# Feed-forward weights in 256-KB pieces, column form for any group, and a new written-out order

## The chip, the core and the metric

The kernel runs on one core of one Trainium2 chip. The metric is the device time of one execution in microseconds. PE is TensorE (matrix products), ACT is ScalarE, DVE is VectorE, POOL is GpSimd, and SP is the queue from which the large loads and stores are issued. A matrix product is two instructions, a load of the stationary operand and the matmul.

## The reference

A transformer block with conditioning: six modulation vectors come from `c`, then attention with 32 query heads and one shared key and value head, then a gated feed-forward, each behind a layer norm. S = 2048 positions, D = 1024, F = 3584, heads of 32, in bf16.

```python
mod = (_silu(c) @ w_mod).reshape(c.shape[0], 6, 1, -1)     # sa, ca, ga, sb, cb, gb
h = _layernorm(x) * (1 + ca) + sa
q = (h @ wq) in 32 heads of 32;  k = h @ wk;  v = h @ wv   # one k and v for all heads
p = softmax(q k^T / sqrt(32));   x = x + ga * ((p v) @ wo)
h = _layernorm(x) * (1 + cb) + sb
x = x + gb * ((_silu(h @ w1) * (h @ w3)) @ w2)
```

## The kernel before

**Tiling.** The positions are cut into 8 blocks of 256 (`NB`), the heads into 8 groups of four. For each block and each group of heads 8 *score groups* (`s_exp`) are made: eight matmuls of 32 rows write a pair of key tiles for four heads into four PSUM banks, and ACT takes the exponential of each half (128x1024), from a ring of three pairs of banks into `U`. There are 512 score groups and 1,024 exponentials. `av` multiplies them by V (128x32 tiles, "A" form), DVE adds them up for the denominators (`pairs`, into `PS`), and `dens` and `attend` divide. When a block has all its heads, `wo` projects it and adds it to `X1`, a layer norm follows, and for blocks 2 to 6 a DMA transpose on SP turns the result around.

**Feed-forward.** `ffn1` runs over 14 slabs of 256 columns of w1 and w3. `slab_dma` loads both parts of a slab from SP into one of three slots (`W13SL`; two of them lie in `W13`, one in `HT`), `slab` multiplies them with the block's layer norm output; ACT takes a tanh, DVE forms the gated product into `HHT`. `ffn2` runs over four quarters of 256 output columns: `w2_dma` loads 28 x 128 rows of w2 into one of two slots (`W2S`; for the last block's third and fourth quarter into `QT` and `U`), `quarter` makes 56 products. All feed-forward weights are loaded again for each of the eight blocks. The feed-forward of one block lies between the score groups of the next; after the last score group only products of the last blocks are left.

**Forms of a product.** A 128x128 product can be issued whole ("F") or as four products of 32 columns at four column positions ("C", four times the instructions). A change between score form "S", narrow forms "A" and "C", and F costs PE some time; A and C go together. In the kernel before, products of `slab`, `q_proj` and `wo` may take form C: `mode_of` gives it when PE stands in A or C, at most `COLS` (12) products after the last A and while an estimated instruction load stays under `FULL`. All pairs of products that go to one group share one list `form`, so the first pair decides for the group. `quarter` has form F alone.

**Order.** `program` builds a graph of operations with their reads and writes. `Placer` puts them on engines; `ORDER` lists all operations by number, so each engine's instruction order is fixed in the text (a "b" marks the second of two possible engines), and each engine waits for semaphores where an operation depends on another engine. The times in `Placer` (`SWITCH`, `LAT` and others) then decide only which PSUM bank a group takes and whether filler matmuls are put into expected gaps of PE.

Of the kernel before, what the change touches and what calls it, by code (L numbers as in the profile page):

```python
# [8 lines left out]
P = 128  # L9
# [110 lines left out]
6 1 11 0 4 2 5 8 3 7 9 12 13 10 25 16-18 59 22 15 14 60 19 61 28 21 62 412 63 27 20 23 64 24 65 26 29 68 30 31 36 45  # L120
37 32 66 33 38 69 39 40 103 67 34 102 41 35 70 104 131 105 71 123 42 72 132 73 122 106 74 43 124 112 107 46 125 44
133 75 126 47 48 134 108 49 135 50 76 136 111 109 127 113 77 137 128b 114 110b 115 129 116 130 117b 78 118 79 80 119
99 172 81 82 171 97 55b 54 53 51 85 58 98b 57 52b 56 173 163 83 86b 174 162 175 138 84 164 182 87 176 139 88 165 89
143 90 166 91 92 142 167 93 94 168 95 183 140 96 144 460 152 145 141b 120 146 151 461 169 153 147 121 462 154 148b
463 155 170b 464 149 156 184 242 185 157b 150 186 177b 421 191 465 187 158 243 192 178 159 193 188b 466 194 179b 195
467 160 202 196 468 197b 469 180 161 470 203 198 181 471 204 472 199b 205 189 473 206 211 100 190b 207 474 475 101
208b 227 477 228 212 229 230 200 476 231 213 244 214 209 215 201b 245 478 246 210 216 232 233 247 234 235 217b 479
222 236 223 248 224 225 480 218 249 226 481 219 250 252 253 251 254 255 487 482 257-260 483 256 501 261 220 502 485
237 503 504 221 238 488 239 505 240 262 263 506 241 484 507 491-493 489 494 508 264 265 509 495 510 266 496 497 511
486 498 499 267 268 512 500 513 490 269 514 270 526 307 515 516 308 517 271 309 310 525 518 519 272 520 311 273 274  # L130
528 521 522 275 523 527 302 303 524 276 562 304 563 305 529-531 564 565 306 532 533 566 541 538 539 567 277 540 568
542 534 543 569 535-537 544 278 570 548 571 553 545 572 546 552 279 547 280 573 549 574 550 297 281 575 298 551 299
# [4 lines left out]
640 646-648 661 649 652 650 662 357 663 680 358 359 664 651 665 360 681 666 327 361 328 667 653 668 654 332 669 333  # L137
682 334 670 335 655 671 336 329 672 330 683 322 673 331 674 323 675 684 324 325 676 677 326 337 678 338 685 413 679
703 414 430 339 418 704 417 415 340 416 686 688 705 706 689 690 707 687 691-693 341 694 708 695 709 699 696 710 697
# [8 lines left out]
834 835 930 836 931 1313 840 1314 828 837 1315 457 411 838 1316 839 1317 458 841 1318 842 843 846-848 1319 459 1320  # L148
# [3 lines left out]
911-913 1369 1335 914 915 1370 916 1336 917 918 890 1383 919 972 891 892 1371 1372 893 920 894 895 1373 896 1340 897  # L152
921 951 922 1338 898 1375 1374 923 899 924-926 1341 1376 927 928 900 1342 973 901 1377 902 1378 1386 903 904 1379
905 906 929 907 1380 952 1406 908 1351 1408 1381 932-934 1407 935 936 1352 937 938 1387 939 1392 940 993 1354 1393
1384 1409 1394 1355 1410 1395 1396 941 1397 1398 1411 1399 1356 1412 1388 942 1413 943-945 1402 946 1414 947 1389
1415 948 1382 949 1416 953 1390 994 954-956 1417 950 1418 957 1385 958 1419 959 960 844 1432 963 1014 964 961 965
1421 1420 966 962 967 968 1433 969 1422 970 974 1391 1015 975 976 1423 971 1424 977 978 845 1425 979 1435 980 981
984 982 1035 985 1427 1426 1436 986 987 983 988 989 1428 990 991 995 992 1036 996 1429 997 1455 1400 1456 998 1401
999 1000 1430 1001 1457 1002 1016 1056 1017 1458 1437 1003 1018 1019 1459 1020-1022 1004 1023 1460 1461 1431 1077
1441 1442 1024 1403 1443 1434 1444 1462 1445 1025 1446-1448 1404 1463 1464 1438 1005 1006 1465 1007 1405 1008 1439  # L160
1009 1010 1466 1011 1451 1467 1440 1012 1468 1026 1481 1057 1027-1030 1469 1470 1013 1031 1032 1471 1482 1033 1037
1078 1038 1034 1039 1472 1040 1473 1041 1474 1042 1484 1043 1044 1047 1045 1098 1048 1476 1475 1485 1049-1051 1046
1052 1477 1053 1054 1058 1055 1099 1059 1478 1060 1504 1449 1505 1061 1450 1062 1063 1479 1064 1506 1065 1507 1119
1490 1452 1491 1066 1492 1453 1493 1508 1494 1067 1495 1496 1454 1497 1509 1510 1500 1068 1486 1069 1511 1070-1073
1512 1074 1487 1513 1075 1488 1514 1079 1120 1080 1081 1076 1082 1083 1515 1480 1516 1084 1085 1517 1483 1086 1089
1140 1090 1489 1091 1087 1092 1519 1518 1088 1093-1095 1530 1520 1096 1100 1141 1101 1102 1521 1103 1097 1522 1104
1531 1105 1523 1106 1107 1533 1110 1161 1111 1108 1525 1524 1112 1109 1113-1115 1534 1526 1116 1117 1121 1118 1162
1122 1527 1123 1553 1498 1124 1554 1499 1125-1127 1501 1128 1555 1502 1556 1738 1503 1539 1540 1129 1528 1541 1542
1557 1543-1545 1130 1546 1558 1559 1549 1131 1529 1132 1560 1133 1134 1532 1135 1136 1561 1535 1562 1137 1138 1563
1142 1739 1143 1139 1144 1145 1564 1536 1565 1146 1147 1537 1566 1148 1149 1579 1152 1759 1153 1150 1154 1155 1567  # L170
1568 1151 1156 1157 1538 1158 1569 1159 1163 1160 1760 1164 1165 1570 1571 1580 1547 1166 1572 1548 1167-1169 1550
1170 1551 1573 1574 1780 1552 1173 1174 1577 1171 1175 1176 1575 1177-1179 1172 1180 1576 1781 1600 1181 1183 1184
1601 1578 1185-1187 1583 1188 1602 1603 1585 1586 1604 1581 1587-1590 1605 1606 1582 1591 1592 1607 1189 1596 1190
1584 1191 1192 1608 1609 1593 1594 1610 1193 1595 1194-1196 1611 1597 1598 1612 1197 1624 1198 1613 1199-1202 1614
1599 1615 1625 1203 1204 1616 1626 1205-1208 1617 1209 1618 1627 1210 1619 1214 1211 1244 1215-1217 1620 1212 1621
1628 1218 1219 1622 1220-1223 1629 1623 1647 1224 1225 1648 1226 1630 1227 1632 1633 1649 1650 1631 1634 1635 1651
1636-1639 1652 1653 1643 1228 1229 1654 1230 1231 1640 1641 1655 1671 1656 1232 1233 1657 1234 1235 1672 1236 1237
# [229 lines left out]
7223 7264-7270 7273 7271 7274-7276 7272 7277 7289 7278-7288 7290  # L407
# [1271 lines left out]
```

## Time and profile before

| | |
|---|---|
| median of 3 runs | 1134.99 us (1133.73 to 1135.88) |
| profiled execution, first to last instruction | 1132.8 us |
| TensorE clock granted | 1.000 |
| PE busy | 1104.8 us (98%), 16,642 matmuls |
| ACT busy | 1021.8 us (90%), of it 967.5 in 1,024 exponentials |
| DVE busy | 983.7 us (87%) |
| loads | 209.16 MB in all, 185 GB/s over the span |

The profiled execution's own time is its span; it lies 2.2 us under the median of the runs. Busy time counts an instruction from start to end, and PE and ACT overlap the end of one with the start of the next, so a busy share near 100% does not say that nothing could be packed closer. Start times of equal instructions in a row give their price. Rows of instructions name what is written and read: `S<-QT,KT` is a score group, `U<-S` an exponential, `PB<-U,V` values, `PB<-QT,W` and `PB<-QT,HT` slabs, `PB<-W2S,HT` quarters; 128\*32 is a narrow form, 128\*128 the full one.

### The profile page before, as it was taken

What the parts mean: (1) busy time and instruction counts of PE and PEld (TensorE: products, weight loads), DVE (VectorE), ACT (ScalarE), POOL (GpSimd) and SP (SyncE); (2) the same over time, 40 slices, a digit from 0 to 9 for tenths busy, and PEclk for the clock granted to TensorE, in tenths of its full rate; (3) what the DMA queues carried; (4) which work ended last, traced back from release to release, by engine and by line L of the source; (5) the groups of instructions that cost most, each with busy time, mean ns of one, the idle gap of its engine ahead of it and who ended that gap; (6) DMA issues with size and microseconds to landing.
All of it is one profiled execution on the core that took longest, in us unless ns stands there. A gap on an engine that the chain in (4) does not pass through costs nothing.

```text
span 1132.8 us, 36935 instructions
## 1 busy us (share of the span) xinstructions
PE 1104.8 (98%) x16642; PEld 754.1 (67%) x16642; DVE 983.7 (87%) x1615; ACT 1021.8 (90%) x1160; POOL 41.0 (4%) x92
## 2 busy tenths in 40 slices
PE   6999999999999999999999999999999999999998
PEld 5744546766567766777577766776567756776887
DVE  7998999897889889998999899998999999997442
ACT  5999999999999999999999999999999999994110
POOL 4300000000000000000000000000000010000000
PEclk9999999999999999999999999999999999999999
DMA  9321487664476675965496577868597557777893
GB/s 345 108 76 32 155 217 202 197 191 110 123 224 196 174 195 150 247 193 154 122 290 197 144 190 193 236 196 217 141 253 215 160 148 194 219 204 196 235 240 105
DMA packets 379429, 209.16 MB, mean 185 GB/s; under 512 B 15488, under 2 KB 371072, under 8 KB 379264
## 3 DMA queue, kind: packets, MB, share of 16 engines
q1 hardware_dynamic: 378832, 206.59, 65.8%
q8 instruction: 132, 2.16, 0.8%
q14 instruction: 33, 0.27, 0.1%
q10 hardware_dynamic: 432, 0.13, 0.0%
HBM read 199.89 MB, written 4.19 MB: 180 GB/s over the span
## 4 chain that ended last, share of the span: by engine, by line
ACT 46%; PE 43%; DVE 6%; DMA 3%; issue 1%; SPq 1%; POOL 0%; DVEq 0%
ACT U L22 44%; PE PB L22 31%; PE S L22 13%; ACT HT L22 3%; DVE PS L22 2%; DMA W<-in_A_wq_dram 1%; DVE ST L22 1%; DMA W2S<-in_B_w_dram 1%; DVE HT L22 1%; SPq L22 1%; DMA W<-in_B_w_dram 1%; DVE X L22 0%; POOL RS L22 0%; DVE QT L22 0%; DVE RB L22 0%
## 5 line engine op out<-in xcount | busy, mean ns | idle before, releaser
L22 ACT ACTIVATE U<-S 128x1024 bf16<-128x1024 f32 x1024 | 967.5, 1143 | 5.3 <-PE S L22 3.9
L22 DVE TENSOR_TENSOR PS<-U 128x2048 bf16<-128x2048 bf16 x256 | 309.1, 1213 | 16.6 <-ACT U L22 14.8
L22 DVE TENSOR_TENSOR PS<-PS 128x1024 bf16<-128x1024 bf16 (+1 forms) x401 | 272.4, 690 | 4.2
L22 PE MATMUL PB<-QT,W 128*128 128x256 bf16 (+1 forms) x2448 | 228.4, 273 | 0.6 <-DVE QT L22 0.5
L22 PE MATMUL S<-QT,KT 32*128 32x256 bf16 x4096 | 203.7, 273 | 7.4 <-ACT U L22 4.7
L22 PEld LDWEIGHTS PB<-QT,W 128*128 128x128 bf16 (+1 forms) x2448 | 169.3, 97 | 43.5 <-issue 22.8
L22 PE MATMUL PB<-W2S,HT 128*128 128x256 bf16 x1512 | 190.2, 273 | 0.0
L22 PEld LDWEIGHTS PB<-W2S,HT 128*128 128x128 bf16 x1512 | 136.9, 98 | 42.2 <-issue 24.0
L22 PEld LDWEIGHTS S<-QT,KT 32*128 32x128 bf16 x4096 | 60.9, 92 | 135.2 <-ACT U L22 115.3
L22 PE MATMUL PB<-U,V 128*32 128x256 bf16 x4096 | 128.7, 273 | 0.6 <-ACT U L22 0.5
L22 PE MATMUL PB<-QT,HT 128*128 128x256 bf16 (+1 forms) x1248 | 116.5, 273 | 1.2 <-issue 1.1
L22 PEld LDWEIGHTS PB<-U,V 128*32 128x32 bf16 x4096 | 101.4, 96 | 23.1 <-issue 13.3
L22 PE MATMUL PB<-HT,W 128*32 128x512 bf16 (+2 forms) x800 | 100.0, 338 | 0.9 <-DVE HT L22 0.9
L22 PEld LDWEIGHTS PB<-QT,HT 128*128 128x128 bf16 (+1 forms) x1248 | 85.1, 97 | 22.0 <-issue 11.7
L22 ACT ACTIVATE HT<-PB 128x512 bf16<-128x512 f32 (+1 forms) x106 | 79.5, 750 | 3.6 <-PE PB L22 3.4
L22 DVE SCALAR_TENSOR_TENSOR HT<-HT,PB 128x512 bf16<-128x512 bf16 x99 | 67.6, 683 | 7.4 <-ACT HT L22 6.3
L22 DVE TENSOR_TENSOR HT<-HT,PB 128x512 bf16<-128x512 bf16 x100 | 68.2, 683 | 5.5 <-PE PB L22 4.4
L22 PEld LDWEIGHTS PB<-HT,W 128*128 128x128 bf16 (+1 forms) x800 | 50.1, 97 | 32.9 <-issue 11.5
L22 ACT ACTIVATE HT<-S 128x512 bf16<-128x512 f32 (+1 forms) x17 | 11.8, 696 | 61.6 <-PE S L22 61.6
L22 PE MATMUL PB<-WO,QT 128*128 128x512 bf16 x224 | 55.7, 381 | 0.0
L22 DVE STREAM_TRANSPOSE RB<-PB 128x256 f32<-128x256 f32 x63 | 28.0, 445 | 25.6 <-PE PB L22 25.5
L22 POOL TENSOR_SCALAR RS<-MV 128x1 f32<-128x1 f32 x32 | 12.3, 387 | 1002.3 <-DVE MV L22 774.8
(119 smaller groups left out, 680.9 us busy)
## 6 DMA issues: line engine op xcount, KB each, us to landing
W<-in_B_w_dram SPq DMA_DIRECT2D x150, 512.0 KB, 4.9
W2S<-in_B_w_dram SPq DMA_DIRECT2D x30, 1792.0 KB, 8.4
HT<-in_B_w_dram SPq DMA_DIRECT2D x74, 512.0 KB, 4.8
W2S<-in_w_mod_dram SPq DMA_DIRECT2D x8, 1024.0 KB, 6.4
X<-in_A_x_dram SPq DMA_DIRECT2D x8, 512.0 KB, 6.7
U<-in_w_mod_dram SPq DMA_DIRECT2D x4, 1024.0 KB, 12.1
out_dram<-X SPq DMA_DIRECT2D x7, 512.0 KB, 8.2
W2S<-in_A_x_dram SPq DMA_DIRECT2D x5, 512.0 KB, 12.2
```

The costliest lines, as they stand in the source:

```text
L22: return getattr(e, call[0])(*call[1], **call[2])
```

## The change

Four things change together.

1. `slab_dma` cuts each load of w1 and w3 into two pieces of 256 KB (four 128-row tiles of the contraction each), `w2_dma` each load of w2 into seven pieces of 256 KB. A pair of products waits for its own piece alone.
2. On SP, every load or store of 256 KB or more that is placed after the first score group waits until the fourth one before it has landed.
3. Each pair of products in `slab`, `q_proj` and `wo` chooses its form for itself, the limits on form C are gone, and `quarter` may use it too. A "b" in the order now marks a pair that takes form F.
4. `ORDER` is new throughout (7,710 operations instead of 7,294, 416 of them the added pieces), and so are constants of `Placer`, which now also estimates when PE's instructions are fetched (`fetched`). Since the order is fixed, these estimates reach the program only through banks and filler.

```diff
-    SWITCH = {"F": 0.095, "S": 0.11, "A": 0.106, "C": 0.106}
+    SWITCH = {"F": 0.072, "S": 0.147, "A": 0.092, "C": 0.092}
...
-    COLS = 12
-    FULL = 36.0
+    COLS = 99
+    FULL = 1e9
...
+    BLOCK = 256
+    AHEAD = 64
+    EXTRA = 1.0083
+    QUEUED = 0.5
+    FOUND = 1.05
+    LANDED = 2.6
+    OPEN = 4
+    LARGE = 1 << 18
...
                 i, k = self.order[len(g.nodes) - left]
                 assert g.nodes[i].npred == 0
+                if k and g.nodes[i].col is not None:
+                    g.nodes[i].col[1][0], k = "F", 0
...
+        if e == "sp" and self.counts(n):
+            if len(self.large) >= self.OPEN:
+                n.preds.setdefault(self.large[-self.OPEN], False)
+            self.large.append(n)
...
+    def counts(self, n):
+        return self.step and n.dma is not None and n.nbytes >= self.LARGE and n.bw > 2e5
+
+    def fetched(self, fn, sess, r, start):
+        count = 2 * len(fn(sess.bank) if sess is not None else fn())
+        self.pc += count * self.EXTRA
+        self.seen = max(self.seen, r)
+        if self.near is None and self.pc >= self.edge - self.AHEAD:
+            self.near = start
+        if self.pc >= self.edge:
+            if self.asked is not None:
+                busy = max([f for s, f in self.loads if s <= self.asked + 0.2] + [0.0]) - self.asked
+                if self.step:
+                    start = max(start, self.asked + max(self.FOUND, self.QUEUED * busy) + self.LANDED)
+            self.asked = max(self.near, self.seen)
...
         def slab_dma(n, s, vt):
             r = (n * NSLAB + s) % NW
             for m, w in enumerate((w1_in, w3_in)):
-                dma("sp", W13SL[r][:, m], w[:, s * 256:(s + 1) * 256].rearrange("(c p) f -> p c f", p=P), ("W13", r, m),
-                    1 << 19, writes=[("W13", r, m)], vt=vt)
+                for h in range(2):
+                    dma("sp", W13SL[r][:, m, 4 * h:4 * h + 4],
+                        w[h * 512:(h + 1) * 512, s * 256:(s + 1) * 256].rearrange("(c p) f -> p c f", p=P), ("W13", r, m, h),
+                        1 << 18, writes=[("W13", r, m, h)], vt=vt)
...
+        PIECE = [(i, i + 4) for i in range(0, NF, 4)]
...
-            dma("sp", w2, w2_in[:, q * 256:(q + 1) * 256].rearrange("(c p) f -> p c f", p=P), key, NF * P * 512,
-                writes=[key], vt=vt)
+            src = w2_in[:, q * 256:(q + 1) * 256].rearrange("(c p) f -> p c f", p=P)
+            for i, (a, z) in enumerate(PIECE):
+                dma("sp", w2[:, a:z], src[:, a:z], key + (i,), (z - a) * P * 512, writes=[key + (i,)], vt=vt)
...
-                        op("pe", full, pe_mm(B, 2), reads=[("W13", r, m)] + h2k(n)[c0:c0 + 2], writes=[("gu", m, n, s)],
-                           vt=vt + 0.01 * m, mode="F", sess=ss[m], post=0.145, col=(cols, form))
+                        op("pe", full, pe_mm(B, 2), reads=[("W13", r, m, c0 // 4)] + h2k(n)[c0:c0 + 2], writes=[("gu", m, n, s)],
+                           vt=vt + 0.01 * m, mode="F", sess=ss[m], post=0.145, col=(cols, [None]))
...
-                    op("pe", lambda b, t=t, f0=f0: [lambda e, f=f: e.matmul(
-                        BANK[b][:, t * B:(t + 1) * B], HHT[:, f, t * P:(t + 1) * P], w2[:, f, :], start=(f == 0),
-                        stop=(f == NF - 1)) for f in range(f0, f0 + 2)], pe_mm(B, 2),
-                       reads=[key] + [("HHT", x) for x in range(f0 // 2, (f0 + 1) // 2 + 1)],
-                       writes=[("f2", n, q, t), ("f2", n, q)], vt=vt, mode="F", sess=s, post=0.145)
+                    full, cols = prods([(
+                        lambda b, y, z, t=t: BANK[b][y:z, t * B:(t + 1) * B],
+                        lambda y, z, t=t, f=f: HHT[:, f, t * P + y:t * P + z],
+                        lambda f=f: w2[:, f, :], f == 0, f == NF - 1) for f in range(f0, f0 + 2)])
+                    op("pe", full, pe_mm(B, 2), reads=[key + (f0 // 4,)] + [("HHT", x) for x in range(f0 // 2, (f0 + 1) // 2 + 1)],
+                       writes=[("f2", n, q, t), ("f2", n, q)], vt=vt, mode="F", sess=s, post=0.145, col=(cols, [None]))
```

More of the change, by code (lines that the diff above doesn't have):

```diff
@@ new lines @@
+1309 1731-1733 2265 1734 1735 2266 1736 1310 1737 1311b 2268 1738 1312-1314 2267 1742 1728 2269 2270 1315 1739 2271
+2272 1316 1740 1317b 1318 2274 1741 1743 1319 1744 1745 1327 1322 1325 1324 1813 1323 1838 1837 1791 1814 1839 1815
+1321 1326 1816 1753 1754 1769 2273 2275-2277 1755 1756b 1770 2278-2280 2287 1757 1283 2281 1771 1748b 1772 2283
+1749-1751 2282 2284 2288 2286 1773 1752 1759 1758 2285 2307-2309 1764 1765b 2290 2291 2310 2311 2292 2293 1766 1767
+2294 2313 2295-2297 2289 1768 2303 1774 1760 845 1775 1776 2312 2314 2315 1328 1329b 2316 2298 1330 1331 2299 2300
@@ new lines @@
+2166-2168b 2619 2169b 2621 2170b 2171b 3164 2172 2622 2173 2174b 2175 3165 3166 2176 2177 3167 2634 3168 3169
+2178-2180 2635-2637 3170 2638-2641 2181 2624 2625 2596 2626-2628 2597 2630 2631 2598 2629 2148 2632 2644 2633 3171
+3172 2182 3173 2183b 2193b 2194-2197 3174 2184 3175 3176 2642 2198 3177 2199-2203 3179 2204b 2205b 3178 2206 2207b
+3180 2208 2209 3182 3181 3183 3184 3188 2185 3190 2643 3191 3189 3193 2645 3192 2646 2647 2210-2212 2655b 2213b 3185
+2214b 2215 2216b 2217 2218b 2656 3186 2223 2228 2692 2227 2715 2229 2741 2224 2694 2226 2739 2225 3187 3213 2219 2220b
@@ new lines @@
+3774 3775 4289 3776 3777 3778b 3779 4288 4290 3780b 3788 3789 3781b 3782 4317 3790b 3791b 3786 3928 3807 3809 3787
+3810 3925 3831 3959 3808 3833 3830 3832 4291 4265 4294 3783 4292 4266 4295 4318 4319 3792 3793 3794b 3795 4320
+4303-4305 3796 4306 4321 4307-4310 4322-4324 4267 3797 4313 4299 4298 4293 4300 4325 3811 3812b 3813b 3798 3814 3799
+3800b 4326 3801 3802 3815b 3803 3804 3805b 4327-4329 3806 4296 4301 4330 3816-3818b 3834b 3835-3837 3838b 4332 3839b
+3819 4331 4333 3820 4302 4343 3840 3821b 3841b 3822b 3922 3854 3856 3927 3853 3876 3842 4334 3843 3823 3824b 3825b
@@ new lines @@
+5873b 5874 6895 6878 6896 6897 5875 5876 6879-6881 6898 6882 5877 6883 6884 5878 6885 6899 6900 6316 6888 6315
+6317-6320 6322 6321 6901 5879 5880b 6902 5881b 5882 6327 5883 6328b 6904 6329-6331b 6332 6333b 6334b 6903 6905 6906
+6335 5884 6875 6873 6871 6336 6337 6338b 6339b 6907 6340 6341 6342b 6908 6909 6343 6344b 6350 6910 6351b 6352
+6353-6355b 6356 6357b 6911 6912 6358 6918 6345 6876 6359 6877 6360b 6361b 6362 6363b 6913 6364-6366 6367b 6373 6374
+6368 6914 6915 6375 6941 6886 6376-6378 6942 6887 6279 6943 6379 6380 6927 6944 6928 6929 6381 6930 6945 6931-6933
@@ L438, in __init__ @@
         self.dma_cnt = {}
-        self.t = {e: 0.0 for e in self.ops}
+        self.t = {e: 1.2 if e == "sp" else 0.0 for e in self.ops}
         self.mode = None
@@ L443, in __init__ @@
         self.run_of = None
+        self.pc = 64.0
+        self.edge = self.BLOCK
+        self.near = None
+        self.asked = None
+        self.seen = 0.0
+        self.loads = []
+        self.large = []
         self.t_s = 0.0
@@ L554, in choose @@
                     r = bt
+            if e == "sp" and self.counts(n) and len(self.large) >= self.OPEN:
+                r = max(r, self.large[-self.OPEN].fin)
             b = t + self.SWITCH.get(self.mode, 0.0) if e == "pe" and self.switches(n) else t
@@ L591, in commit @@
             self.keep_on(before, start)
+        if e == "pe":
+            mode = self.mode_of(n)
+            start = self.fetched(n.col[0] if mode == "C" and n.col is not None else fn, s, r, start)
         if e == "sp" or n.dma is not None:
@@ L595, in commit @@
             n.fin = self.bw + 0.5
+            self.loads = self.loads[-11:] + [(start, n.fin)]
         else:
@@ L629, in commit @@
         self.free_pending()
+    def counts(self, n):
[12 more added lines that the diff above has]
+            self.asked = max(self.near, self.seen)
+            if self.step == 0 and self.bw > self.asked:
+                self.bw += 1.1
+            self.near = None
+            self.edge += self.BLOCK
+        return start
     def keep_warm(self, start):
@@ L891, in full @@
         def full(b=None):
-            return [lambda e, o=o, w=w, x=x, st=st, sp=sp: e.matmul(o(b, 0, P), w(0, P), x(), start=st, stop=sp)
+            return [lambda e, o=o, w=w, x=x, st=st, sp=sp: e.matmul(o(b, 0, P), w(0, P), x(), start=st, stop=sp, skip_group_check=True)
                     for o, w, x, st, sp in lst]
@@ L923, in dma @@
             return n
-        FAST = 370e3
+        FAST = 386e3
         def pc(ap):
@@ L1128, in q_proj @@
             s = Sess()
-            form = [None]
             hk = [("HT", cc, tt) for cc in range(NC) for tt in range(2 * n, 2 * (n + nn))]
@@ L1138, in q_proj @@
                 op("pe", full, pe_mm(w, 2) * cold, reads=wk + hk, writes=[("q", n, f)], vt=vt, mode="F", sess=s, post=0.145,
-                   col=(cols, form))
+                   col=(cols, [None]))
             op("dve", lambda b: [lambda e: e.tensor_scalar(
@@ L1386, in wo @@
                     s = Sess()
-                    form = [None]
                     for q in range(4):
@@ L1395, in wo @@
                            reads=[(k, *i) for f in range(2 * q, 2 * q + 2) for k, i in (("QT", (n, f)), ("WOG", (f,)))],
-                           writes=[("wo", n, t, h)], vt=vt, mode="F", sess=s, post=0.145, col=(cols, form))
+                           writes=[("wo", n, t, h)], vt=vt, mode="F", sess=s, post=0.145, col=(cols, [None]))
                     xs = X1[:, n % NX, t, h * 512:(h + 1) * 512]
@@ L1444, in w2_dma @@
             if key == ("W2X", 0):
-                G.alias([key], [("QT", b, f) for b in range(4) for f in range(NC)])
+                G.alias([key + (i,) for i in range(NF // 4)], [("QT", b, f) for b in range(4) for f in range(NC)])
             elif key == ("W2X", 1):
-                G.alias([key], [("U", m, i) for m in range(NU) for i in range(2)])
-            dma("sp", w2, w2_in[:, q * 256:(q + 1) * 256].rearrange("(c p) f -> p c f", p=P), key, NF * P * 512,
-                writes=[key], vt=vt)
+                G.alias([key + (i,) for i in range(NF // 4)], [("U", m, i) for m in range(NU) for i in range(2)])
+            src = w2_in[:, q * 256:(q + 1) * 256].rearrange("(c p) f -> p c f", p=P)
+            for i, (a, z) in enumerate(PIECE):
+                dma("sp", w2[:, a:z], src[:, a:z], key + (i,), (z - a) * P * 512, writes=[key + (i,)], vt=vt)
         def ffn1(n, vt0, vt1):
@@ L1462, in slab @@
                 for sub in range(2):
-                    form = [None]
                     for c0 in range(0, NC, 2):
@@ L1588, in program @@
         G.alias([("HHT", s) for s in range(NSLAB)] + [("H20", cc) for cc in range(NC)] +
-                [("W13", 2, m) for m in range(2)] + [("TS", r) for r in range(2)] + [("O2B", r, t) for r in range(2) for t in range(2)], ht)
-        G.alias([("W13", r, m) for r in range(2) for m in range(2)], ["WQ0", "WQ1"])
-        G.alias([("W2S", r) for r in range(2)], [("XS", tt) for tt in range(6, NTT)] + [("WMB", 0), ("WMB", 1)])
+                [("W13", 2, m, h) for m in range(2) for h in range(2)] + [("TS", r) for r in range(2)] + [("O2B", r, t) for r in range(2) for t in range(2)], ht)
+        G.alias([("W13", r, m, h) for r in range(2) for m in range(2) for h in range(2)], ["WQ0", "WQ1"])
+        G.alias([("W2S", r, i) for r in range(2) for i in range(NF // 4)], [("XS", tt) for tt in range(6, NTT)] + [("WMB", 0), ("WMB", 1)])
         for n in range(NB):
```

542 lines of the change are left out of this document (297 added, 245 removed), and 43 rows, old and new, of the table ORDER.

## The prediction

> **What bounds the kernel now.** I read the page first, then busy time by stage, then instructions in order of time for the price of one product, one change of array form and one exponential, and last the waits and the loads. The page: two engines are full, and the chain that ended last runs over both.
>
> ```profile
> span 1132.8 us, 36935 instructions
> PE 1104.8 (98%) x16642; PEld 754.1 (67%) x16642; DVE 983.7 (87%) x1615; ACT 1021.8 (90%) x1160; POOL 41.0 (4%) x92
> ACT 46%; PE 43%; DVE 6%; DMA 3%; issue 1%; SPq 1%; POOL 0%; DVEq 0%
> ```
>
> By stage (columns: PE, PEld, DVE, ACT, POOL busy, granted clock, DMA share, GB/s) PE and ACT are both busy to 99% while there are scores; after 1030 us PE is alone.
>
> ```profile
> 510.00:670.00 160.00, 159.56 (x2457) 109.22 (x2450) 146.75 (x233) 159.07 (x181) 1.97 (x4) 1.00 0.68 185
> 670.00:830.00 160.00, 159.38 (x2390) 107.25 (x2389) 149.13 (x247) 159.25 (x182) 4.77 (x8) 1.00 0.76 200
> 1030.00:1133.00 103.00, 98.89 (x932) 84.37 (x931) 44.20 (x82) 10.88 (x17) 1.76 (x4) 1.00 0.77 204
> ```
>
> Busy shares hide slack here, so I price the work by start times. PE in order of time (start, length, what):
>
> ```profile
> 30.47 0.40 PE L22 MATMUL S<-QT,KT 32*128 32x256 bf16 x8
> ...
> 509.36 0.40 PE L22 MATMUL S<-QT,KT 32*128 32x256 bf16 x8
> 509.68 0.29 PE L22 MATMUL PB<-PS,ONES 128*32 128x256 bf16 x4
> 509.80 2.79 PE L22 MATMUL PB<-QT,HT 128*32 128x256 bf16 x96
> 512.56 0.40 PE L22 MATMUL S<-QT,KT 32*128 32x256 bf16 x8
> 512.89 1.48 PE L22 MATMUL PB<-W2S,HT 128*128 128x256 bf16 x12
> 514.31 0.40 PE L22 MATMUL S<-QT,KT 32*128 32x256 bf16 x8
> 514.64 1.48 PE L22 MATMUL PB<-W2S,HT 128*128 128x256 bf16 x12
> ...
> 522.06 0.29 PE L22 MATMUL PB<-PS,ONES 128*32 128x256 bf16 x4
> 522.29 1.48 PE L22 MATMUL PB<-W2S,HT 128*128 128x256 bf16 x12
> ...
> 1030.04 0.40 PE L22 MATMUL S<-QT,KT 32*128 32x256 bf16 x8
> ```
>
> The 12 products from 512.89 last to 514.31: 1.42 us, that is 12 x 0.109 and 0.11 for the change into the score form. A score group with the change out of it takes 0.33 (514.31 to 514.64), so 0.44 with both changes. The 96 narrow matmuls are 24 products in column form: 2.76 us less the 0.11 is 0.110 a product, no dearer than full form, but with four pairs of instructions instead of one. From column to full form: 0.23 (522.06 to 522.29) less 0.11 of work is 0.12.
>
> ACT in order of time:
>
> ```profile
> 503.91 3.03 ACT L22 ACTIVATE U<-S 128x1024 bf16<-128x1024 f32 x3
> 506.64 0.79 ACT L22 ACTIVATE HT<-PB 128x512 bf16<-128x512 f32 x1
> 507.12 3.98 ACT L22 ACTIVATE U<-S 128x1024 bf16<-128x1024 f32 x4
> ```
>
> An exponential steps by 0.91 (2.73/3) and a tanh by 0.48. The 511 steps from the first score group at 30.47 to the last at 1030.04 took 999.6 us. With these prices the work between them, counted in the kernel's own order, is 978.6 us on PE and 981.5 on ACT (1,022 exponentials, 98 tanh and five of the layer norms' and K's). So neither bounds alone: a stretch costs the larger of the two plus what their coupling wastes, because a score group cannot start before older exponentials have emptied its banks. In 16 stretches of 32 score groups the larger of the two sums to 989.2; the other 10.4 us are lost inside the stretches. After the last score group stand 98.8 us of PE work.
>
> **The change, part by part.** The new order is written out in the diff, so its forms and its work can be counted as well.
>
> Forms. Each pair of products now takes column form whenever PE stands in a narrow form, unless the order marks it. The trace of before has 400 products in column form:
>
> ```profile
> L22 PE MATMUL PB<-HT,W 128*32 128x512 bf16 x320 | 20.7, 380 | 0.0
> L22 PE MATMUL PB<-QT,W 128*32 128x256 bf16 x832 | 25.4, 273 | 0.0
> L22 PE MATMUL PB<-QT,HT 128*32 128x256 bf16 x448 | 14.0, 273 | 0.0
> ```
>
> (1,600/4). The new order gives 714, of which 348 belong to the second feed-forward product, which had none. The changes between narrow and full form, counted over the whole timeline, fall from 85 to 61: 24 x 0.12 = 2.9 us of PE work gone. The 512 score groups keep their two changes each.
>
> Order. Counted at the same prices, PE's work between first and last score group falls from 978.6 to 974.4 (2.9 by forms, the rest moved behind the last score group), ACT's stays at 981.5, and the larger of the two, in 16 stretches, sums to 983.7 instead of 989.2: 5.5 us less, since the PE-heavy stretches (63.4, 63.5, 63.0, 63.6, 63.2 us against 62.6 on ACT) come down to 61.9 to 62.8. The 10.4 us lost within stretches I keep. That is the largest term and the least sure: nothing if ACT alone sets the pace (the upper bound), and -7 if 1.5 us of the inner loss go as well (the spread of PE's work per score group falls from 0.284 to 0.275 us). Taken: -5.5.
>
> Tail. Behind the last score group stand 374 instead of 358 products of the second feed-forward product, less some changes of form: 100.3 against 98.8 us. Nothing runs beside PE there: +1.5.
>
> Pieces. Two loads of 512 KB a slab become four of 256, one of 1792 KB a quarter becomes seven. PE itself waited for weights only twice, both in the tail, and twice for nothing shown:
>
> ```profile
> PE S L22 <- DMA W2S<-in_B_w_dram: 0.6, 1, 0.6
> PE S L22 <- DMA W<-in_B_w_dram: 0.5, 1, 0.5
> PE PB L22 <- issue: 1.1, 2, 0.9
> ```
>
> The first product now waits for 256 KB alone, so I take both weight waits away: -1.1; at worst they stay. SP issues 723 loads instead of 307, 416 x 0.37 us (below) = 154 us on a queue that idles most of the span: 0 while a piece moves in 0.9 us (262,144 B at 293 GB/s) and is issued in 0.37.
>
> ```profile
> 1062.96 0.37 SPq L22 DMA_DIRECT2D HT<-in_B_w_dram  x1
> W<-in_B_w_dram SPq DMA_DIRECT2D x150, 512.0 KB, 4.9
> W2S<-in_B_w_dram SPq DMA_DIRECT2D x30, 1792.0 KB, 8.4
> out_dram<-X SPq DMA_DIRECT2D x7, 512.0 KB, 8.2
> QT<-XNB SPq DMA_TRANSPOSE x10, 3.1
> 1055.00:1060.00 5.00, 5.00 (x48) 4.47 (x47) 0.69 (x1) 0.60 (x1) 0.00 (x0) 1.00 1.19 293
> ```
>
> The wait. Each load of 256 KB or more on SP waits for the fourth one before it. Behind it in SP's queue stand the next pieces, the ten transposes (the next block's feed-forward waits for them) and the stores. A store of 512 KB is one of the four and lands after 8.2 us, so the queue can stand for 8.2 - 3 x 0.9 = 5.5 us, seven times. In the middle the new order leaves a piece a median of 14 us of PE work between its slot coming free and its first use, which hides that: 0; without this cover 5.5 us each.
>
> Code. 132 packets of 2.16 MB are 256 instructions of 64 B each:
>
> ```profile
> q8 instruction: 132, 2.16, 0.8%
> 315.90 0.39 PE L22 MATMUL PB<-QT,HT 128*128 128x256 bf16 x2
> 317.16 1.03 PE L22 MATMUL PB<-QT,HT 128*128 128x256 bf16 x8 [0.86 <-issue]
> ```
>
> That is the one clear stop without a releaser inside the score stage; it follows narrow matmuls and fits code that came late behind big loads. The new order has some 1,880 instructions more (314 products x 3 x 2), and stretches of 256 that hold less than 5.2 us of PE work rise from 8 to 19. On the other side at most 1 MB of weights is queued ahead of a fetch. Bounds: -1.1 (no such stop left) to 11 x 0.86 = +9.5. Taken: 0, because 8 tight stretches gave only two stops.
>
> By the Trainium skill (Runtime: NRT & Kernel Launch, "Instruction fetch mechanics") code comes in 16 KiB blocks of 256 instructions and crossing a block is mostly hidden; by that rule the third rival below cannot happen and counting the fetches brings nothing. The packet size agrees; the stop of 0.86 us does not look hidden.
>
> Head: the same nine loads precede the first weights of Q, so the first score group stays at 30.5: 0 (half a microsecond either way, three of eight scalings of those weights on POOL instead of two).
>
> Sum: -5.5 + 1.5 - 1.1 + 0 = -5.1 on the profiled 1132.8. The median of the runs is 1134.99, 2.2 above the span, which I keep: 1129.9, rounded **1130.0**.
>
> **The rivals.** (1) ACT alone sets the pace, and PE's relief becomes waiting: ACT's 981.5 us are equal in both orders, and it is 99% busy in every stage. Against it: five stretches hold more work on PE. Then the phase stays, +1.5 - 1.1 remain: 1135.4, no change. (2) Slower: four pieces in flight don't fill the queues in the tail. The new order needs 22.0 MB (84 pieces) in 87.4 us of PE work there, 252 GB/s (in its hardest stretch 12.6 MB in 49.5 us, 254; before 10.5 MB in 41.8, 251). Now the tail reaches 293 when there is enough queued. But 1.05 MB in flight that land in 4.9 us, as two loads of 512 KB do, are 214 GB/s: 22.0 MB then take 102.8 us, 15.4 too long. It decides from 252 GB/s down; at 230 it costs 95.7 - 87.4 = 8.3 us: 1138.3. For a loss: the 4.9. Against: a 256-KB piece needs less time behind its predecessors, 3 x 0.9 us.
>
> The Trainium skill speaks for this rival (DMA: Bandwidth & Descriptors, "Rules for kernel authors"): full bandwidth wants at least 1 MiB in a DMA. No row here has a 256-KB load; if the rule held for each piece alone the time would be the rival's 1138.3 or more.
>
> (3) Slower: the denser narrow stretches run out of code, at 0.86 us for each of the 11 more: 1139.5.
>
> **How the numbers follow.** Forecast 0.58, ACT alone 0.20, starved tail 0.14, late code 0.08. The forecast's own range is 1125 to 1132.5: the inner loss too on one side, half of the order's gain on the other. All cases: 1123 to 1140, which leaves out the worse half of both slower rivals. A measurement tells 0.2% (2.3 us) from no change, so: faster 0.58, same 0.20, slower 0.22.
>
> **What would show it.** First to last score group 994 us instead of 999.6, last score group at about 1024.5, and 104 us behind it; changes of form 61; PE's two waits for weights gone; landings of 256 KB at 3.5 to 4.5 us and some 290 GB/s in the tail; about 138 code packets, and PE's idle "issue" about 1. Wrong if the phase keeps its 999.6 (rival 1), if PE waits for W or W2S for microseconds (2), or if "issue" grows to 5 or more (3).

## The result and the profile after

The change made the kernel slower: 1146.76 us (median of 5 runs, 1143.92 to 1149.57) against 1134.93 us (5 runs), a ratio of 1.0111 (95% interval 1.0094 to 1.0127). The prediction said 1130.0, between 1123 and 1140. The profiled execution took 1147.8 us from first to last instruction; it is the longest of the five, 1149.57 us, so its waits are on the high side. From its page: span, PE, code packets, the chain that ended last by engine and by line.

```profile
span 1147.8 us, 39292 instructions
PE 1109.5 (97%) x17544; PEld 754.1 (66%) x17544; DVE 967.4 (84%) x1615; ACT 1022.2 (89%) x1159; POOL 42.9 (4%) x93
...
q8 instruction: 140, 2.29, 0.8%
...
PE 48%; DMA 24%; ACT 19%; DVE 6%; SPq 1%; issue 1%; POOL 1%; DVEq 0%
PE PB L22 36%; ACT U L22 18%; PE S L22 11%; DMA W<-in_B_w_dram 9%; DMA W2S<-in_B_w_dram 6%; DMA HT<-in_B_w_dram 6%; DVE PS L22 2%; ACT HT L22 1%; DMA W<-in_A_wq_dram 1%; SPq L22 1%; POOL RS L22 1%; DVE ST L22 1%; DVE QT L22 1%; DVE X L22 1%
```

In the chain DMA went from 3% to 24%, and 21 of these points are the feed-forward weights. PE's waits (columns: us in all, times, the longest) say the same:

```profile
PE PB L22 <- DMA W<-in_B_w_dram: 6.5, 8, 1.6
PE PB L22 <- DMA HT<-in_B_w_dram: 5.0, 4, 3.1
PE S L22 <- ACT U L22: 3.7, 9, 0.9
...
PE PB L22 <- DMA W2S<-in_B_w_dram: 1.2, 3, 0.6
...
PE S L22 <- DMA W<-in_B_w_dram: 0.7, 2, 0.4
...
PE S L22 <- DMA HT<-in_B_w_dram: 0.4, 1, 0.4
```

Before, PE waited 1.1 us for feed-forward weights; now 6.5 + 5.0 + 1.2 + 0.7 + 0.4 = 13.8. No row "issue" is among PE's waits. The first and the last score group on the timeline of the changed kernel:

```profile
30.38 0.40 PE L22 MATMUL S<-QT,KT 32*128 32x256 bf16 x8
...
1040.75 0.40 PE L22 MATMUL S<-QT,KT 32*128 32x256 bf16 x8
```

The score phase takes 1010.4 us (before 999.6; predicted 994), and 107.0 follow it (before 102.8; predicted 104). Its loads land in 4 us each:

```profile
W<-in_B_w_dram SPq DMA_DIRECT2D x300, 256.0 KB, 4.1
W2S<-in_B_w_dram SPq DMA_DIRECT2D x210, 256.0 KB, 4.0
HT<-in_B_w_dram SPq DMA_DIRECT2D x148, 256.0 KB, 4.0
...
out_dram<-X SPq DMA_DIRECT2D x7, 512.0 KB, 4.0
```

Four pieces in flight are 1.05 MB; landing in 4.0 to 4.1 us they are 256 to 262 GB/s (an estimate), if SP issues the next one the moment one has landed.

### The profile page after: what moved, and what is told of

It is laid out like the page before. It is cut to its first block, busy times and chain, and to the rows that moved or that the text cites. A ratio compares the mean times of both kernels' runs of the same rounds, so it can differ in the third digit from the quotient of the medians.

```text
span 1147.8 us, 39292 instructions
## 1 busy us (share of the span) xinstructions
PE 1109.5 (97%) x17544; PEld 754.1 (66%) x17544; DVE 967.4 (84%) x1615; ACT 1022.2 (89%) x1159; POOL 42.9 (4%) x93
## 4 chain that ended last, share of the span: by engine, by line
PE 48%; DMA 24%; ACT 19%; DVE 6%; SPq 1%; issue 1%; POOL 1%; DVEq 0%
PE PB L22 36%; ACT U L22 18%; PE S L22 11%; DMA W<-in_B_w_dram 9%; DMA W2S<-in_B_w_dram 6%; DMA HT<-in_B_w_dram 6%; DVE PS L22 2%; ACT HT L22 1%; DMA W<-in_A_wq_dram 1%; SPq L22 1%; POOL RS L22 1%; DVE ST L22 1%; DVE QT L22 1%; DVE X L22 1%; DVE HT L22 1%
## 5 line engine op out<-in xcount | busy, mean ns | idle before, releaser
L22 DVE TENSOR_TENSOR PS<-PS 128x1024 bf16<-128x1024 bf16 (+1 forms) x401 | 267.7, 688 | 1.8
L22 PE MATMUL PB<-QT,W 128*128 128x256 bf16 (+1 forms) x2378 | 241.5, 273 | 5.2 <-DMA W<-in_B_w_dram 4.2
L22 PE MATMUL PB<-W2S,HT 128*32 128x256 bf16 (+1 forms) x2500 | 191.1, 273 | 1.5 <-DMA W2S<-in_B_w_dram 1.2
L22 PEld LDWEIGHTS PB<-W2S,HT 128*32 128x32 bf16 (+1 forms) x2500 | 137.3, 97 | 34.9 <-issue 19.2
L22 PE MATMUL PB<-U,V 128*32 128x256 bf16 x4032 | 139.4, 274 | 0.7 <-DVE RB L22 0.5
L22 PE MATMUL PB<-QT,HT 128*128 128x256 bf16 (+1 forms) x1320 | 131.2, 274 | 5.2 <-DMA HT<-in_B_w_dram 5.0
L22 PEld LDWEIGHTS PB<-U,V 128*32 128x32 bf16 x4032 | 97.4, 96 | 28.9 <-issue 17.7
L22 PEld LDWEIGHTS PB<-QT,HT 128*128 128x128 bf16 (+1 forms) x1320 | 90.2, 98 | 27.8 <-issue 9.3
L22 PE MATMUL PB<-HT,W 128*128 128x256 bf16 (+2 forms) x650 | 102.1, 328 | 2.8 <-DMA W<-in_B_w_dram 2.3
L22 PE MATMUL PB<-WO,QT 128*128 128x512 bf16 (+1 forms) x288 | 60.6, 380 | 0.0
```

Of the source, the lines that this page charges most:

```text
L22: return getattr(e, call[0])(*call[1], **call[2])
```

## The experiments

All in one table. "Phase" is from the first score group to the last on the timeline, "behind" from there to the end of the span. "Waits" is PE's waiting for feed-forward weights. These three come from one profiled execution each, whose time need not be the median (for e6 it was the shortest, 1138.70), so they can be off by a microsecond or two.

| kernel | median us | ratio to before, 95% interval | phase | behind | waits |
|---|---|---|---|---|---|
| before | 1134.93 | | 999.6 | 102.8 | 1.1 |
| after | 1146.76 | 1.0111 (1.0094 to 1.0127) | 1010.4 | 107.0 | 13.8 |
| e1 no limit | 1141.61 | 1.0044 (1.0029 to 1.0059) | 1003.8 | 105.9 | 5.4 |
| e2 limit of eight | 1141.63 | 1.0057 (1.0041 to 1.0074) | 1003.5 | 105.8 | 4.4 |
| e3 old order, pieces | 1133.26 | 0.9981 (0.9972 to 0.9991) | 999.4 | 101.5 | 0 |
| e4 the same, limit of four | 1135.08 | 1.0000 (0.9990 to 1.0009) | 999.3 | 102.7 | 1.5 |
| e5 no limit, SP sorted | 1139.12 | 1.0034 (1.0020 to 1.0048) | 999.5 | 107.1 | 1.8 |
| e6 limit of four, SP sorted | 1140.71 | 1.0048 (1.0031 to 1.0065) | 996.3 | 110.0 | 3.8 |
| e7 e3 with free forms | 1133.27 | 0.9984 (0.9974 to 0.9994) | 999.6 | 101.4 | 0 |
| e8 e5, half loads | 1133.94 | 0.9992 (0.9982 to 1.0002) | 997.7 | 103.4 | 0 |
| e9 e3, half loads | 1134.02 | 0.9989 (0.9979 to 0.9998) | 999.9 | 101.5 | 0 |
| e10 e8, short exponentials | 1121.45 | 0.9878 (0.9862 to 0.9895) | 985.5 | 103.6 | 0 |
| e11 e9, short exponentials | 1125.77 | 0.9920 (0.9904 to 0.9937) | 990.9 | 101.5 | 0 |

**Is it the limit of four loads?** e1 takes the added wait out and keeps everything else; e2 waits for the eighth load before.

```diff
         if e == "sp" and self.counts(n):
-            if len(self.large) >= self.OPEN:
-                n.preds.setdefault(self.large[-self.OPEN], False)
+            # e1: nothing;  e2: if len(self.large) >= 8: n.preds.setdefault(self.large[-8], False)
             self.large.append(n)
```

> The changed kernel without the wait for the fourth load before (order, pieces, forms, banks and filler untouched). Theory A, the wait starves the queues: in the profiled run of the changed kernel PE waited 13.8 us for feed-forward weights and four pieces in flight landed in 4.17 us, which is 251 GB/s, against 252 to 265 that the order needs in its dense stretches. Without it those waits fall under 3 us, the tail reaches 290 GB/s and the time comes to 1128 to 1136. Theory B, a 256-KB load is dear in itself: waits stay over 8 us, 1142 to 1147. Theory C, the new order itself is worse (its loads stand in a bad order on SP, or its products do): 1140 to 1147 with the waits for weights mostly there or replaced by waits for ACT. Theory D, code comes late: 1146 or more, with more idle time under issue, since more bytes are queued ahead of a fetch.

> The changed kernel with the wait for the eighth load before instead of the fourth. Theory A: 2.1 MB in flight are enough to fill the queues, so the time is within 2 us of the kernel without the wait, 1128 to 1137. Theories B and C: unchanged, 1142 to 1147.

Without the wait 5 us come back, with eight in flight as many. So with this order four are too few and eight are enough, but both kernels are still slower than before. Both lie in the range of theory C and outside that of theory A.

**Is it the pieces?** e3 gives before's order and forms the 256-KB pieces without a limit (the w2 loads are cut in the same way); e4 adds the wait for the fourth.

```diff
-                dma("sp", W13SL[r][:, m], w[:, s * 256:(s + 1) * 256]..., ("W13", r, m), 1 << 19, ...)
+                for h in range(2):
+                    dma("sp", W13SL[r][:, m, 4 * h:4 * h + 4], w[h * 512:(h + 1) * 512, ...]..., ("W13", r, m, h), 1 << 18, ...)
...
+            # e4 alone: n.preds.setdefault(self.large[-4], False)
```

> The kernel before, with its own order and forms, its feed-forward loads cut into 256-KB pieces (each load's pieces one after the other at the load's old place on SP), no wait for earlier loads. Theories A and C: the pieces cost nothing or save the two weight waits of 1.1 us: 1133 to 1136. Theory B: 1140 or more.

> The same old order with pieces, and with the wait for the fourth load before. Theory A: its dense stretches need 250 to 260 GB/s, four in flight give about 250, so 3 to 10 us are lost, mostly in the tail: 1137 to 1145. Theory C (the limit is harmless, the new order is at fault): 1133 to 1136, as without the wait.

Page of e3 and its busy time in the middle of the tail:

```profile
span 1131.4 us, 37358 instructions
...
W<-in_B_w_dram SPq DMA_DIRECT2D x300, 256.0 KB, 4.1
W2S<-in_B_w_dram SPq DMA_DIRECT2D x210, 256.0 KB, 4.6
HT<-in_B_w_dram SPq DMA_DIRECT2D x148, 256.0 KB, 4.0
```

```profile
1060.00:1105.00 45.00, 45.00 (x415) 40.34 (x413) 19.57 (x29) 7.76 (x13) 0.00 (x0) 1.00 1.04 282
```

The same stretch of the kernel before:

```profile
1060.00:1105.00 45.00, 44.52 (x408) 39.62 (x407) 18.59 (x28) 7.77 (x13) 0.00 (x0) 1.00 0.94 250
```

The pieces alone make the kernel faster, by 0.2%: PE waits for no weight, and the 256-KB loads move 282 GB/s while PE is never idle. The limit takes that gain away again (e4: 256 GB/s in the same stretch), but it costs 1.8 us and not the 3 to 10 of theory A. A 256-KB load is not dear in itself, so theory B is out. By the Trainium skill (DMA: Bandwidth & Descriptors, "Rules for kernel authors") full bandwidth wants at least 1 MiB in a DMA. No run here tests that for 256 KB: in its first 28 us, with loads of up to 1.5 MB, e3 moves 346 GB/s, more than the 282. What the runs show is that 256-KB loads feed this stretch, and better than loads of 512 KB and 1792 KB did (250).

So the rest of the loss, some 8 us between e1 and e3, belongs to the new order with its forms, banks and filler; e7 below takes the forms out of that.

**What in the order?** One stop of the changed kernel, first on PE, then on SP's queue (start, length, load):

```profile
383.11 0.39 PE L22 MATMUL PB<-QT,W 128*128 128x256 bf16 x2
386.58 2.31 PE L22 MATMUL PB<-QT,HT 128*128 128x256 bf16 x10 [3.08 <-DMA HT<-in_B_w_dram]
```

```profile
377.80 1.15 SPq L22 DMA_DIRECT2D W<-in_B_w_dram  x2
379.32 0.37 SPq L22 DMA_DIRECT2D W2S<-in_B_w_dram  x1
380.31 0.37 SPq L22 DMA_DIRECT2D HT<-in_B_w_dram  x1
381.12 0.37 SPq L22 DMA_DIRECT2D W<-in_B_w_dram  x1
385.06 0.37 SPq L22 DMA_DIRECT2D HT<-in_B_w_dram  x1
```

The piece that PE waits for is the one issued at 380.31; it landed at 386.54. The last product that used its slot was through at 368.7, so the load could have been issued 11.6 us earlier. But SP issues in the order of its list. Ahead of it stood pieces for slots that came free later (the two of 377.80 only at 373.4 and 376.0) and pieces that were needed much later (the W2S piece of 379.32 at 411.0), and each of them waited for its fourth predecessor. Over all pieces, a free slot waited 5.9 us (median) for its load to be issued; 4.8 in e1, 0.05 in e3.

e5 and e6 change only that: e1 and the changed kernel with SP's list sorted, each piece at the place where its slot comes free. The sequences of the other engines stay.

```diff
-ORDER = """ ... """      # SP's loads where the changed kernel has them
+ORDER = """ ... """      # 657 of them moved, by up to 62 places forward and 18 back
-    GAP = 0.7
+    GAP = 99.0            # keeps PE's sequence: no filler for gaps that the planner now expects
```

> The changed kernel without the wait for the fourth load (as e1_no_limit), and with SP's list of loads sorted anew: each 256-KB piece stands where the products of e1_no_limit free its slot, earliest first use ahead among those that are free. The sequences of PE, ACT, DVE and POOL and all forms are those of e1_no_limit. In e1_no_limit a free slot waited 4.8 us (median) before SP issued its load, in e3_old_order_pieces 0.05 us. Theory (SP stands at loads whose slot is still in use, in front of loads whose slot is free): PE's waits for W, W2S and HT fall from 4.9 us together to under 1.5, time 1133 to 1136 us. Rival (the new order of products asks for weights faster than they come, or loses in short stops that are no weight waits): 1139 to 1142 us as e1_no_limit.

> e5_sorted_fetches with the wait for the fourth load put back, so the changed kernel with nothing but SP's list sorted anew. Theory (two separate losses: SP's order, and four pieces in flight that bring 251 GB/s): 1136 to 1140 us, PE's weight waits 3 to 7 us instead of 13.8. If the limit only hurts because SP's order is bad: 1133 to 1136 us, within 2 us of e5_sorted_fetches. If SP's order is not a cause: 1145 to 1148 us.

PE's waits for weights in e5, and in e6:

```profile
PE PB L22 <- issue: 1.6, 1, 1.6
PE S L22 <- DMA W<-in_B_w_dram: 1.6, 3, 1.2
...
PE PB L22 <- DMA HT<-in_B_w_dram: 0.2, 1, 0.2
```

```profile
PE S L22 <- DMA W<-in_B_w_dram: 2.1, 3, 1.0
...
PE S L22 <- DMA HT<-in_B_w_dram: 1.0, 1, 1.0
PE PB L22 <- DMA HT<-in_B_w_dram: 0.7, 1, 0.7
```

With SP's list alone changed, e6 has 3.8 us of weight waits instead of 13.8 and is 6.0 us faster than the changed kernel, and no run of the one overlaps a run of the other. The limit then costs 1.6 us (e6 less e5) instead of 5.1; the runs of e5 and e6 overlap, so this is no more than "2 us or less", which fits a limit that hurts because of SP's order. The time of e6 lies just above the 1136 to 1140 of its theory. But e5 missed its 1133 to 1136 and lies in the range of the rival, at 1139.12. Against e1 it gains 2.5 us, which is not clear of the noise (the ratios to the kernel before are 1.0034 and 1.0044, with overlapping intervals). In e5 the phase is back at 999.5, and what is left is the tail: 107.1 behind the last score group against 101.5 in e3. Whether the rival's first half is the reason, weights asked for faster than they come, is what e8 tests.

**Do the forms pay?** e7 gives e3 the free forms: the changed kernel's code without the limit, with before's order and a mark at each pair of products that takes form F.

```diff
-                   ... mode="F", sess=s, post=0.145, col=(cols, form))
+                   ... mode="F", sess=s, post=0.145, col=(cols, [None]))    # also in quarter
```

> The order of the kernel before, 256-KB pieces, no wait for the fourth load (as e3_old_order_pieces), and the form of each pair of products chosen by itself, also in the second feed-forward product: changes between narrow and full form 85 to 30, which at the prediction's prices takes 5.2 us out of PE's content. Theory that the prediction's price of forms is right and PE sets part of the pace: 1129 to 1131.5 us, 2 to 4 us under e3_old_order_pieces (1133.3). Rival that ACT alone sets the pace of the score phase: 1132.5 to 1134 us, no change against e3_old_order_pieces outside the tail.

The trace has the 30 changes, PE's content falls by 5.2 us at the prediction's prices, and the time does not move (1133.27 and 1133.26; phase 999.6 and 999.4). That is the rival's range: the relief was not on the path.

**What do the transfers cost, and what the order without them?** e8 and e9 let each load bring half its piece (the w2 loads too); the other half of the weights is left out.

```diff
-                    dma("sp", W13SL[r][:, m, 4 * h:4 * h + 4], w[h * 512:(h + 1) * 512, ...]
+                    part = 4 if n == 0 else 2
+                    dma("sp", W13SL[r][:, m, 4 * h:4 * h + part], w[h * 512:h * 512 + part * P, ...]
```

> e5_sorted_fetches, but from the second 256-row block on each weight load brings only the first half of its piece (128 KB, two of four chunks); the products read what the slot held before. All sequences but SP's transfers stay, and every product runs. It prices the weight transfers in the new order. Theory (the new order gains in the score phase, where ACT is busy 993.3 of 999.5 us and leaves at most some 3 us to win, and gives more back behind the last score group, where PE waits some 3.5 us for pieces): phase 996 to 998 us, tail 103 to 104 instead of 107.0, time 1132 to 1135 us. Rival (transfers are not the reason for the longer tail): tail stays at 106 to 107, time 1137 to 1139. If the prediction's term for the order is right once fetches are cheap: phase 994 to 995, time 1129 to 1131.

> Control for e8_sorted_half_loads: e3_old_order_pieces with the same half loads (128 KB of each 256-KB piece from the second block on). There PE has no wait for weights, so less data should change nothing: phase 999.5, tail 101.4, time 1132.5 to 1134 us. If it gets faster too, half loads help by something that is no weight wait (less traffic for all), and e8's gain has to be read against this one.

Last score group and busy time by stage, of e8 and then of e9 (ACT is the fourth busy column, GB/s the last):

```profile
1028.16 0.40 PE L22 MATMUL S<-QT,KT 32*128 32x256 bf16 x8
```

```profile
30.50:1030.00 999.50, 984.03 (x16288) 652.75 (x16323) 901.24 (x1475) 994.66 (x1128) 26.66 (x47) 1.00 0.39 111
```

```profile
1030.32 0.40 PE L22 MATMUL S<-QT,KT 32*128 32x256 bf16 x8
```

```profile
30.50:1030.00 999.50, 983.68 (x15406) 653.75 (x15433) 916.42 (x1478) 992.87 (x1126) 24.44 (x46) 1.00 0.40 111
```

All three ranges of e8's theory are met, and the control e9 gained nothing from half loads. With cheap transfers the new order is as fast as the old one (1133.94 and 1134.02): it wins 2.2 us in the phase and gives 1.9 back in the tail, where it has 16 products more. With full transfers its tail is 3.7 us longer still (107.1 less 103.4); in the old order they cost nothing (101.5 in e3 and e9). In the tail of e5 the products fall 3.2 us behind the same products of e8 between 1081 and 1104 us, in short stops; the list shows 1.8 of that as waits for pieces, since it counts only what lies behind the end of the product before. The phase of e5 is 1.8 us longer than that of e8; e5's single stop of 1.6 us without a releaser ("issue", above) is nearly all of it.

**Does ACT set the pace of the phase?** e10 and e11 shorten ACT's work, in both orders, with the half loads.

```diff
-                        S6[:, 2 * r[i]:2 * r[i] + 2, :], ACT.Exp, scale=SCALE)]
+                        S6[:, 2 * r[i]:2 * r[i] + 2, 0:448 if c > 15 else 512], ACT.Exp, scale=SCALE)]
```

> e8_sorted_half_loads, and from the 17th score group on each exponential covers 896 instead of 1024 columns (the rest of its tile keeps older values), so that ACT has about an eighth less work in the score phase. All other engines' sequences stay. To be read against e11_old_half_short_exp, which is the same for the old order. Theory (in both orders ACT sets the pace of the score phase, which is why 4 us less PE content bought only 2): the phase becomes PE's, falls to 978 to 986 us here, and 3 to 5 us under that of e11. Rival (ACT isn't the pace; the new order loses its content in short PE stops): the phase falls by under 5 us from 997.8, or lies within 1 us of e11's.

> e9_old_order_half_loads with the same short exponentials as e10_sorted_half_short_exp. Theory (ACT sets the pace): the phase falls from 1000.0 to 982 to 990 us, that is to PE's own content (978.6 by the prediction) and a few us of stops, 3 to 5 us above e10's. Rival: falls by under 5 us, or within 1 us of e10's.

Last score group of e10, and of e11:

```profile
1015.79 0.40 PE L22 MATMUL S<-QT,KT 32*128 32x256 bf16 x8
```

```profile
1021.07 0.40 PE L22 MATMUL S<-QT,KT 32*128 32x256 bf16 x8
```

With shorter exponentials both phases fall, by 12.2 us (to 985.5) and 9.0 us (to 990.9), and the new order is now 5.4 us ahead of the old one instead of 2.2. So ACT held both phases back (by its work or by when it frees the banks, which these runs do not tell apart), and it hid 3.2 us of what the new order saves on PE. It did not do so alone: the shortest step of an exponential falls from 0.904 to 0.796 us, some 107 us over the 992 shortened ones, and no more than 12 of them come out; after that ACT waits for PE's scores. The row of e11's exponentials says so (behind the bar busy time and mean ns, then ACT's idle time before them and what ended it):

```profile
L22 ACT ACTIVATE U<-S 128x896 bf16<-128x896 f32 x992 | 854.4, 920 | 55.9 <-PE S L22 46.9
```

The old order's 990.9 lies a little above the 982 to 990 that were expected, and the 5.4 above the 3 to 5.

## Why the prediction was wrong

Three terms failed: the wait, taken as 0; the feeding of the weights, taken as 0 too; and the order's gain, taken as 5.5. From the forecast up, along the medians: 1130.0 to 1133.94 with cheap transfers (e8), +3.9, mostly the order; to 1139.12 with full transfers and a good list on SP (e5), +5.2; to 1141.61 with SP's own list (e1), +2.5; to 1146.76 with the limit of four, +5.1. So far as e5 the time would still have been between 1123 and 1140. The runs were made in several sets, in which the kernel before took 1134.93 to 1135.86, so a step of a microsecond is not sure, and the 2.5 by itself is not either. The 7.6 of list and limit together is.

- **The wait, 0: failed, and with SP's list it cost most, 7.6 us.** I took the median of 14 us between a slot's release and its first use as cover. That cover counts only from the time of issue, and a load is issued when everything ahead of it in SP's list has been issued. I never looked at which loads stood ahead. Its two parts, SP's list and the limit, work through each other: with the sorted list the limit costs 1.6; with SP's own, 5.1; with the old list, 1.8 (e4 less e3). The stores, which I had named as the danger, were harmless: 4.0 us to land instead of 8.2.

- **Order, -5.5: failed, through ACT.** With cheap transfers the phase won 2.2 us (e8 against e9). With ACT out of the way the two phases differ by 5.4 (e10 against e11), so there was something to win on PE. That this is so near the 5.5 is luck: for PE by itself my prices give 978.6 less 974.4, 4.2. What failed is the rule that a stretch costs the larger of PE and ACT plus a loss that stays: the new order's 983.7 and 10.4 make 994.1, and e8 took 997.7, a loss of 14.0. Stretches of 32 score groups (from the starts of the exponentials in e9 and e8) show where. The five in which I had more work on PE (63 to 64 us each) came down by 2.7 together. But the five that alternate with them, where I had the larger work on ACT and so counted PE's as free, rose by 2.3; with the short exponentials they rise by 2.4 (e10 against e11), which points to PE work that was moved into them.

I had also read both engines as 99% busy while there are scores. That holds from 350 us on; ahead of it PE is busy to 96% and 98%:

```profile
30.40:190.00 159.60, 152.87 (x2676) 82.71 (x2675) 149.20 (x262) 157.99 (x175) 10.49 (x22) 1.00 0.43 128
190.00:350.00 160.00, 156.06 (x2387) 105.22 (x2385) 138.23 (x216) 159.83 (x184) 1.58 (x4) 1.00 0.61 170
```

Over the whole phase the kernel before shows ACT busy for 993.3 of 999.5 us and PE for 986.6:

```profile
30.50:1030.00 999.50, 986.62 (x15435) 653.18 (x15434) 916.47 (x1478) 993.28 (x1126) 24.51 (x46) 1.00 0.65 178
```

This row does not settle which of them sets the pace. At the shortest steps in the trace (0.904 us an exponential, 0.477 a tanh) ACT's work is some 973 us, so 20 of its 993.3 are short waits that hide where one instruction overlaps the next. The experiments say more: of work taken from PE, 5.2 us brought nothing (e7) and 4.2 brought 2.2 (e8 against e9), while shorter exponentials brought 9 to 12. This comes near rival 1, to which I gave 0.20.

- **Rival 2 (tail starved, 0.14): the direction was right, the criterion and the place were not.** It decided from a mean of 252 GB/s down. In the middle of the tail the changed kernel, and e5 without the limit, moved more than that:

```profile
1060.00:1105.00 45.00, 43.62 (x400) 37.60 (x398) 17.22 (x34) 5.16 (x9) 0.97 (x2) 1.00 0.93 265
```

```profile
1060.00:1105.00 45.00, 42.97 (x383) 36.51 (x382) 14.90 (x24) 6.35 (x11) 0.00 (x0) 1.00 1.03 276
```

and their tails still lost 3.6 and 3.7 us against e8's 103.4, in short stops, of which the list puts 2.1 and 1.8 us down to single pieces that came late. A mean over the tail cannot show that. With the phase, full transfers cost 5.2 us (e5 against e8). In the changed kernel the larger part of the waiting came in the phase, 11.7 of 13.8 us, where I had not looked for it.

- **Tail, +1.5: right** for the products (101.5 to 103.4 with half loads). **Pieces, -1.1: right** in the old order (102.8 to 101.5) and swamped in the new one.

- **Forms, 24 changes fewer: counted right** (85 and 61 changes in the traces), worth nothing in the time, as e7's larger saving shows. The products in column form were counted wrong: before has 416, not 400, since its 64 narrow matmuls `PB<-HT` are 16 more, so the change adds 298 and not 314. Nothing in the sum hangs on it.

- **Code, 0 (rival 3, 0.08): right**, inside wide bounds (-1.1 to +9.5). 140 packets instead of the 138 expected and no stop without a releaser in the changed kernel's waits; single ones of 0.3 to 1.6 us in e1, e2 and e5, whose cause is not shown. **Head, 0: right** (30.38).

Not settled: why the tail of the old order, with nearly as many bytes, is fed without a wait; I did not try the new order's phase with the old order's tail. The gaps of 1 to 3 us between phases of sorted kernels (996.3, 997.7, 999.5) are not explained beyond the one stop in e5.

## What to carry to other kernels

Before a queue's loads are given a limit or a new order, work out for each load when its slot comes free and when it is really issued: cover begins at the issue, and a queue that works in order issues nothing past a load that must wait. Where two engines look equally full, busy shares do not tell which one sets the pace: shorten the work of each in turn and see what comes out (here 0 and 2 us for 5.2 and 4.2 on PE, 9 to 12 for an eighth of ACT's exponentials). And work that is moved from one stretch into another is not free there because another engine has more to do. A change of four parts is better priced one by one: here the pieces alone are worth 0.2% (e3, which with e7 is the fastest whole version), and each of the others cost or brought nothing.

## What the runs showed of the hardware

After some stops PE ran slowly for a time. The stage around the stop of 3.08 us in the changed kernel, and the stage with the slow products in e6 (the granted clock is the number behind POOL's column):

```profile
385.00:390.00 5.00, 3.42 (x23) 1.97 (x24) 1.92 (x3) 0.87 (x2) 0.00 (x0) 0.66 0.39 113
```

```profile
1090.00:1094.00 4.00, 3.84 (x21) 2.65 (x20) 0.00 (x0) 0.00 (x0) 0.00 (x0) 0.57 0.93 264
```

PE's timeline in e6:

```profile
1087.95 0.61 PE L22 MATMUL PB<-QT,HT 128*128 128x256 bf16 x4 [0.68 <-DMA HT<-in_B_w_dram]
1089.61 0.39 PE L22 MATMUL S<-QT,W 128*128 128x256 bf16 x2 [1.04 <-DMA W<-in_B_w_dram]
...
1090.78 0.64 PE L22 MATMUL S<-W2S,HT 128*128 128x256 bf16 x2
1091.21 0.63 PE L22 MATMUL S<-QT,W 128*128 128x256 bf16 x2
...
1093.72 0.38 PE L22 MATMUL PB<-QT,HT 128*128 128x256 bf16 x2
1093.94 0.38 PE L22 MATMUL S<-QT,HT 128*128 128x256 bf16 x2
```

Two products step by 0.43 us from 1090.78 on and by 0.22 again from 1093.72: half the speed for 2.9 us, some 1.5 us lost on top of the waits. The Trainium skill (TensorE: Matmul & The Clock Gate, "What's actually happening") gives half clock after an idle window of about 3.4 us. The stop of 3.08 us comes near that; around the slow products of e6 no wait was longer than 1.04 us and the clock fell all the same, behind three waits of 0.68, 1.04 and 0.16 us within 2.6 us. Nor is a stop always there: in e3 the granted clock was 0.51 from 146.10 to 149.60 us, and PE had no idle time of more than 0.05 us in the 6 us before. So the runs do not show what the condition is. In the changed kernel and in e6 the slow stretch came with late weights, and there it is a cost that the list of waits does not show.
